# Two-layer experts over memory attention: token matmuls with layer-1 columns on partitions, 32x32 VectorE transposes and tiled sums

## The chip, the cores and the metric

The kernel runs on one core of one Trainium2 chip. The metric is the device time of one execution in microseconds (us). The engines are named as in the profile: PE is TensorE's matmul side and PEld its weight load, DVE is VectorE, ACT is ScalarE, POOL is GpSimd, SP the engine that issues all DMAs here.

## The reference, cut to what matters

Three stages follow each other. For 4 batches of 576 tokens, 8 heads of width 64 and 32 memory slots:

```
a    = softmax over tokens of phi                         # [b,h,s,m]
k_m  = a^T k ; v_m = a^T v                                # [b,h,m,d]
attn = softmax over m of (q k_m^T / 8)                    # [b,h,s,m]
x    = attn v_m, heads side by side                       # [2304, 512]
p    = domain_probs / sum                                 # [2304, 4]
x2   = sum over 4 experts e of p[:,e] * (relu(x w1[e]) w2[e])      # w1 512x1024, w2 1024x512
L    = x2 phi2                                            # [2304, 32] logits of 32 slots
d    = softmax of L over tokens ; c = softmax of L over slots
slot = d^T x2                                             # [32, 512]
out  = c (per slot group of 4: relu(slot v1) v2)          # 8 slot experts, v1 512x1024, v2 1024x512
```

Everything is 32-bit. The kernel never forms x or x2. It multiplies v_m into w1 first (G = v_m w1, per batch and 512 of the 4096 layer-1 columns), so that relu(x w1) is relu(attn G) with a contraction of 256; and it multiplies w2 into phi2 (M), so that the logits are h M and the slot inputs are (d^T h) w2, with h the layer-1 outputs times p.

## The kernel before, in words

The order of instructions on every engine is the order in which the Python code issues them. The main loop walks over 4 batches and 8 chunks of 512 layer-1 columns (32 steps). Each chunk is half of an expert.

- `g_half` (L381) makes G for the next step, 256 rows at a time: four matmuls whose results lie on four groups of 32 partitions (column tiles), contraction 128 with half of `vb` zero. ACT writes the rounded value (`hi`), DVE the rest (`lo`).
- `up` (L402) makes h for a tile of 128 tokens: tokens on partitions, 512 columns; six matmuls (A hi x G hi, A hi x G lo, A lo x G hi, for two halves of the contraction) into one of two PSUM banks (`psm`, tag `mm`). A batch has five such tiles; the fifth holds its last 64 tokens beside 64 zero columns. DVE takes the bank out with relu and the token's share p (L423).
- `turn` (L430) turns the previous step's h tile with four TensorE transposes and an ACT copy (L444), since `logits` (L446) needs columns on partitions. `logits` adds up over all 8 chunks of a batch in PSUM.
- `group` (L556) ends a batch: softmax statistics over tokens, transposes back to tokens on partitions (`back`), weighted sums over tokens (`sums`, L620, four column tiles of 32 at a time), and the row softmax for the output (`row_exp`, `row_norm`, `row_turn`).
- `attention(b)` (L789) makes the next batch's `A`, `kbd` and `vb`. Its pieces and those of `group` stand in a list `bg`, from which `pump` takes one entry after each `up`. In batch 0 the steps also hold `m_stages`, which makes M from w2.
- After the last batch come 160 blocks of 256 KB: 32 of w2 again, 64 of v1, 64 of v2. They are fetched in a fixed order (`order`) by SP as slots come free: 56 slots (`blk`), shared with h, G, q, k, v and output tiles, some kept back by `reserve` in the last batch. `fold` and `combine` make the two halves of the output.

Of the kernel before, what the change touches and what calls it, by code (L numbers as in the profile page):

```python
# [16 lines left out]
def kernel(  # L17
# [17 lines left out]

    nc = tc.nc
# [7 lines left out]
    NB = 56  # L44
# [4 lines left out]
    hTp = ctx.enter_context(tc.tile_pool(name="hTp", bufs=1))  # L49
    rawp = ctx.enter_context(tc.tile_pool(name="rawp", bufs=2))  # L50
    blk = ctx.enter_context(tc.tile_pool(name="blk", bufs=NB))
# [10 lines left out]
    live = [0]  # L62

    def block(shape, name, dt=F32):

        live[0] += 1
        assert live[0] <= NB, (name, live[0])
        return blk.tile(shape, dt, tag="b", name=name)

    def spent(n=1):  # L70
        live[0] -= n
        fill()
# [6 lines left out]
    par = const.tile([128, 2], F32)  # L79
# [3 lines left out]
    prob = const.tile([128, 18, E], F32)  # L83
    ct = const.tile([128, 18, 128], F32R)
    A = [const.tile([128, 2, 2, 640], F32R, name=f"A{n}") for n in range(2)]
    kbd = [const.tile([128, 4, 2, NM], F32, name=f"kbd{n}") for n in range(2)]
    vb = [const.tile([128, 2, 128], F32, name=f"vb{n}") for n in range(2)]
    M = const.tile([128, NCH, 4, NSLOT], F32)
    srun = const.tile([128, 2, 512], F32)
# [7 lines left out]
    def load_phi(b):  # L97

        t = att.tile([128, 36, NM], F32, tag="ph", name="ph")
        nc.sync.dma_start(  # L100
            out=t[:, 0:32, :].rearrange("p (h r) m -> p h (r m)", h=H),
            in_=phi[b, :, 0:512, :].rearrange("h (p r) m -> p h (r m)", r=4),
        )
        for c in range(2):
            nc.sync.dma_start(
                out=t[64 * c:64 * c + 64, 32:36, :],
                in_=phi[b, 4 * c:4 * c + 4, 512:576, :].rearrange("i p m -> p i m"),
            )
        ph_t[b] = t

    def load_kv(b, w):

        src = (k, v)[w]
        if w == 0:
            kv_t[b, "t"] = att.tile([128, 2, 4, HD], F32, tag="kt", name="kt")
        t = kv_t[b, "t"]
        for c in range(2):
            nc.sync.dma_start(
                out=t[64 * c:64 * c + 64, w],
                in_=src[b, 4 * c:4 * c + 4, 512:576, :].rearrange("i p d -> p i d"),  # L120
            )
        for c in range(2):
            for ih in range(2):
                t = block([128, 2, 4 * HD], "kv")
                h0 = 4 * c + 2 * ih
                nc.sync.dma_start(
                    out=t,
                    in_=src[b, h0:h0 + 2, 0:512, :].rearrange("i (p r) d -> p i (r d)", r=4),
                )
                kv_t[b, w, c, ih] = t  # L130

    def load_q(b, ti):

        t = block([128, 4, 2, HD], "q")
        for c in range(2):
            if ti < 4:
                nc.sync.dma_start(
                    out=t[:, :, c],
                    in_=q[b, 4 * c:4 * c + 4, 0:512, :].rearrange("i (p r) d -> r p i d", r=4)[ti],
                )  # L140
            else:
                nc.sync.dma_start(
                    out=t[0:64, :, c],
                    in_=q[b, 4 * c:4 * c + 4, 512:576, :].rearrange("i s d -> s i d"),
                )
        q_t[b, ti] = t

    def kv_stages(b):
# [57 lines left out]
        def whole(w, c):  # L206

            def f():
# [3 lines left out]
                for r in range(5):  # L212
                    for i in range(4):
                        o = st[w, c][32 * i:32 * i + 32, 0:64]
                        if r < 4:
                            nc.tensor.matmul(  # L216
                                o, main(c)[:, i, r, :],
                                kv_t[b, w, c, i // 2][:, i % 2, r * HD:(r + 1) * HD],
# [7 lines left out]
                spent(2)  # L226
# [16 lines left out]
        def sk():  # L243
            sums()
            km = att.tile([128, 2, 64], F32, tag="mx", bufs=2, name="km")
            for c in range(2):
# [5 lines left out]
            st["rp"] = att.tile([128, 2, 2], F32, tag="rsp", name="rsp")  # L252
            nc.vector.tensor_tensor(
                out=st["rp"], in0=st["rs"].unsqueeze(2).to_broadcast([128, 2, 2]),
                in1=par.unsqueeze(1).to_broadcast([128, 2, 2]), op=ALU.mult,
            )

# [11 lines left out]
        def vs(c):  # L269
            def f():  # L270
                whole(1, c)()
                if c == 0:
                    st["vm"] = att.tile([128, 2, 128], F32, tag="vm", name="vm")
                for g in range(2):
                    nc.scalar.activation(
                        out=st["vm"][:, c, 64 * g:64 * g + 64], in_=st[1, c][:, 0:64],
                        func=ACTF.Copy, scale=st["rp"][:, c, g:g + 1],
                    )
            return f

        def s6():

            t5 = bank()
            for c in range(2):
                nc.tensor.transpose(t5[:, 128 * c:128 * c + 128], st["vm"][:, c, :], ident)
            nc.scalar.copy(  # L286
                out=vb[b % 2], in_=t5[:, 0:256].rearrange("p (c m) -> p c m", c=2)
            )
# [3 lines left out]
    def q_stages(b, ti):  # L292
# [3 lines left out]
        o = 128 * ti if ti < 4 else 512 + 64 * (b % 2)  # L296

        def s0():
            t = bank()
            for j in range(4):  # L300
                nc.tensor.transpose(
                    t[:, 128 * j:128 * j + n], q_t[b, ti][0:n, j].rearrange("p c d -> p (c d)"),
                    ident[0:n, 0:n],
                )
            spent()
            qt = att.tile([128, 4, 128], F32, tag="qt", bufs=2, name="qt")
# [59 lines left out]

    raw = {}

    def load_w1(s):
        if s >= B * NCH:  # L370
# [8 lines left out]
    G = {}  # L379

    def g_half(s, c):  # L381

        def f():
            b = s // NCH
            t = bank()
            for i in range(4):
                nc.tensor.matmul(  # L387
                    t[32 * i:32 * i + 32, :], vb[b % 2][:, c, 32 * i:32 * i + 32],
# [669 lines left out]
```

## Time and profile before

| | us |
|---|---|
| median of 3 runs (lowest, highest) | 707.61 (706.89, 713.17) |
| the profiled execution | 708.74 |
| its span, first to last instruction | 707.0 |
| PE busy in it | 641.8 |
| DVE busy | 303.0 |
| ACT busy | 198.2 |

The profile is one execution. Times in its views count from the first instruction; a line of a timeline gives start, length, engine, source line, operation, tiles (written <- read), shapes and how many were merged, then in brackets how long the engine had been idle and what ended that. A matmul of 32-bit operands that is not rounded first shows as two records.

### The profile page before, as it was taken

The numbers are of one execution on the slowest core, as the hardware profiler recorded it, in microseconds if no ns is written. First come the engines' busy times: TensorE is split into PE (matmuls) and PEld (weight loads), VectorE is DVE, ScalarE is ACT, GpSimd is POOL, SyncE is SP. The second block draws the span as 40 slices with busy tenths as digits, with TensorE's granted clock in tenths as the row PEclk, the third lists the DMA queues.
The fourth block names the chain that finished last, engine by engine and source line by source line (L and its number), as shares of the span: only waits on it lengthen the run. The fifth ranks groups of instructions, "written<-read, shape, count | busy, mean of one in ns | idle before, by whom it ended". The sixth has DMA issues, their size and how long they took to land.

```text
span 707.0 us, 11204 instructions
## 1 busy us (share of the span) xinstructions
PE 641.8 (91%) x4588; PEld 376.6 (53%) x4588; DVE 303.0 (43%) x655; ACT 198.2 (28%) x438; POOL 2.2 (0%) x11
## 2 busy tenths in 40 slices
PE   7969999999999999899999999999899987899995
PEld 6746675666554566555545566564555553222232
DVE  4576456444443634633345645633533331311012
ACT  1323343333341323323313323322222223010012
POOL 0000000000000000000000000000000000000000
PEclk7999999999999999999999999999999998999997
DMA  7856432331115522111111553232312322999999
GB/s 213 256 171 217 151 127 84 139 136 60 61 61 160 156 76 83 60 60 60 61 59 60 160 158 98 62 117 92 133 60 75 119 62 103 379 404 388 382 382 311
DMA packets 97554, 105.95 MB, mean 150 GB/s; under 512 B 31456, under 2 KB 64736, under 8 KB 97504
## 3 DMA queue, kind: packets, MB, share of 16 engines
q1 hardware_dynamic: 97504, 105.24, 45.0%
q8 instruction: 36, 0.59, 0.3%
q14 instruction: 14, 0.11, 0.0%
HBM read 100.50 MB, written 4.72 MB: 149 GB/s over the span
## 4 chain that ended last, share of the span: by engine, by line
PE 72%; DMA 11%; ACT 8%; DVE 6%; issue 1%; SPq 0%; ACTq 0%; DVEq 0%
PE mm L411 11%; PE mm L412 10%; PE mm L413 10%; DMA v<-in_moe_w_dram 9%; PE at L387 9%; PE at L435 7%; PE lb L454 6%; PE at L620 5%; ACT hT L444 3%; ACT g L392 3%; DMA ph<-in_phi_dram 2%; PE at L316 2%; PE at L478 2%; PE at L216 1%; ACT hTx L444 1%
## 5 line engine op out<-in xcount | busy, mean ns | idle before, releaser
L423 DVE TENSOR_SCALAR h<-mm,prob 128x512 f32<-128x512 f32 (+1 forms) x160 | 119.9, 749 | 159.2 <-PE mm L413 156.3
L411 PE MATMUL mm<-g,A 128*128 128x512 f32 x320 | 142.4, 445 | 0.5 <-ACT A L349 0.5
L412 PE MATMUL mm<-g,A 128*128 128x512 f32 x320 | 126.8, 396 | 0.0
L413 PE MATMUL mm<-g,A 128*128 128x512 f32 x320 | 126.3, 395 | 0.0
L444 ACT COPY hT<-at 128x512 f32<-128x512 f32 x128 | 74.8, 587 | 125.4 <-PE at L435 125.4
L435 PEld LDWEIGHTS at<-ident,h 128*128 128x128 f32 x576 | 66.6, 140 | 62.2 <-issue 38.9
L435 PE MATMUL at<-ident,h 128*128 128x128 f32 x576 | 89.2, 278 | 0.1
L411 PEld LDWEIGHTS mm<-g,A 128*128 128x128 f32 x320 | 60.9, 190 | 33.9 <-issue 12.4
L387 PE MATMUL at<-raw,vb 128*32 128x512 f32 x512 | 68.6, 608 | 0.2 <-ACT vb L286 0.2
L413 PEld LDWEIGHTS mm<-g,A 128*128 128x128 f32 x320 | 60.3, 188 | 14.8 <-DVE A L350 0.2
L392 ACT CAST g<-at 128x512 fp32r<-128x512 f32 x64 | 37.5, 586 | 102.7 <-PE at L387 102.6
L412 PEld LDWEIGHTS mm<-g,A 128*128 128x128 f32 x320 | 61.0, 191 | 8.2 <-issue 0.7
L393 DVE TENSOR_TENSOR g<-at,g 128x512 fp32r<-128x512 f32 x64 | 44.2, 690 | 45.8 <-ACT g L392 45.5
L454 PE MATMUL lb<-hT,M 128*32 128x512 f32 x256 | 34.1, 605 | 22.2 <-ACT hT L444 22.2
L1013 PE MATMUL mm<-v,hz 128*8 128x256 f32 x256 | 35.7, 380 | 3.7 <-DVE mm L937 1.3
L620 PE MATMUL at<-h,dt 128*32 128x512 f32 x288 | 35.2, 630 | 0.3 <-ACT dt L611 0.3
L910 PE MATMUL mm<-v,sT 128*32 128x512 f32 x128 | 28.7, 600 | 0.9 <-DMA v<-in_moe_w_dram 0.5
L484 DVE COPY w2T<-at 128x128 f32<-128x128 f32 x64 | 17.9, 290 | 16.9 <-ACT w2T L486 16.7
L444 ACT COPY hTx<-at 128x512 f32<-128x512 f32 x16 | 9.4, 585 | 53.6 <-PE at L435 53.6
L1013 PEld LDWEIGHTS mm<-v,hz 128*8 128x8 f32 x256 | 8.6, 87 | 27.8 <-DMA v<-in_moe_w_dram 19.2
L316 PE MATMUL at<-kbd,qt 128*128 128x64 f32 (+1 forms) x160 | 19.7, 266 | 3.0 <-ACT qt L307 2.3
L387 PEld LDWEIGHTS at<-raw,vb 128*32 128x32 f32 x512 | 10.1, 108 | 22.9 <-issue 17.1
(145 smaller groups left out, 494.7 us busy)
## 6 DMA issues: line engine op xcount, KB each, us to landing
v<-in_moe_w_dram SPq DMA_DIRECT2D x160, 256.0 KB, 5.4
raw<-in_moe_w_dram SPq DMA_DIRECT2D x32, 1024.0 KB, 5.0
w<-in_moe_w_dram SPq DMA_DIRECT2D x32, 256.0 KB, 5.3
kv<-in_k_dram SPq DMA_DIRECT2D x16, 256.0 KB, 4.3
q<-in_q_dram SPq DMA_DIRECT2D x32, 128.0 KB, 5.0
kv<-in_v_dram SPq DMA_DIRECT2D x16, 256.0 KB, 4.8
out_dram<-ot SPq DMA_DIRECT2D x16, 256.0 KB, 4.1
ph<-in_phi_dram SPq DMA_DIRECT2D x4, 512.0 KB, 6.7
```

What stands on the lines that cost most here:

```text
L387: nc.tensor.matmul(t[32 * i:32 * i + 32, :], vb[b % 2][:, c, 32 * i:32 * i + 32], raw[s][:, 2 * c + i // 2, :], start=True, stop=True,)
L392: nc.scalar.copy(out=hi, in_=t)
L393: nc.vector.tensor_tensor(out=lo, in0=t, in1=hi.bitcast(F32), op=ALU.subtract)
L411: nc.tensor.matmul(ps, ah, gh, start=(c == 0), stop=False)
L412: nc.tensor.matmul(ps, ah, gl, start=False, stop=False)
L413: nc.tensor.matmul(ps, al, gh, start=False, stop=(c == 1))
L423: nc.vector.tensor_scalar(out=hid[T, n][rows], in0=ps[rows], scalar1=0.0, scalar2=prob[rows, T, e:e + 1], op0=ALU.max, op1=ALU.mult,)
L435: nc.tensor.transpose(t[:, 128 * a:128 * a + 128], hid[T, n][:, 128 * a:128 * a + 128], ident)
L444: nc.scalar.copy(out=dst, in_=t.rearrange("p (a t) -> p a t", a=4))
L454: nc.tensor.matmul(lb[key][32 * a:32 * a + 32, 0:w], M[:, n, a, :], src[:, a, :], start=(n == 0), stop=(n == NCH - 1),)
L620: nc.tensor.matmul(t[32 * j:32 * j + 32, :], st["dt"][:, i], hid.pop((T0 + i, 4 * kk + j)), start=(i == 0), stop=(i == nt - 1),)
L1013: nc.tensor.matmul(acc[32 * i:32 * i + 8, :], hz[:, eb, g * fp + f, i, :], use((2, dh, eb, fp, i))[:, n_ * f:n_ * f + n_], start=(k_ == 0 ...
```

## The change

Layer-1 columns go on partitions. `up` now takes 128 columns of G as weights and streams 288 tokens (half a batch, no zero columns) of A: 8 groups of six matmuls a step. ACT takes the bank out with relu into `hT`, which `logits` reads as it is; DVE copies it to `hid` in transposed 32x32 blocks. The share p no longer goes into h: `logits` closes after each expert, DVE transposes its 32x32 blocks, POOL (for the last expert DVE) multiplies by the share and adds up (`expert`), and the weights of the sums get it too (`weights`). `sums` uses 32x32 tiles of TensorE: 4 groups of token rows into 4 PSUM banks, 4 experts on 4 groups of columns. `g_mult` puts the two halves of G on two groups of 64 rows, without zeros. The last batch goes in two halves (`units`), so that its first half's tokens are finished early; the fetches go into whole tiles that become free (`A0`, `ph`, five `big` ones of nine blocks, `A1`, `raw`, `g`), and output tiles share five `hT` slots. Before the first `up`, all of batch 0's q tiles are now done.

```diff
-    blk = ctx.enter_context(tc.tile_pool(name="blk", bufs=NB))
+    gp = ctx.enter_context(tc.tile_pool(name="gp", bufs=2))
+    bigp = ctx.enter_context(tc.tile_pool(name="bigp", bufs=5))
+    units = [(b, ((0, 288), (288, 576))) for b in range(B - 1)]
+    units += [(B - 1, ((0, 288),)), (B - 1, ((288, 576),))]
...
+    def g_mult(s):
...
+        ts = [bank() for c in range(2)]
+        for i in range(4):
+            for c in range(2):
                 nc.tensor.matmul(
+                    ts[c][32 * i:32 * i + 32, :], vb[b % 2][64 * c:64 * c + 64, 32 * i:32 * i + 32],
+                    raw[s][64 * c:64 * c + 64, i, :], start=True, stop=True,
+                )
...
+    def up(u, n, fb, ki):
...
+        ps = mbank()[:, 0:w]
         for c in range(2):
-            nc.tensor.matmul(ps, ah, gh, start=(c == 0), stop=False)
-            nc.tensor.matmul(ps, ah, gl, start=False, stop=False)
-            nc.tensor.matmul(ps, al, gh, start=False, stop=(c == 1))
-        nc.vector.tensor_scalar(
-            out=hid[T, n][rows], in0=ps[rows], scalar1=0.0, scalar2=prob[rows, T, e:e + 1],
-            op0=ALU.max, op1=ALU.mult,
-        )
+            ah, al = A[b % 2][:, c, 0, o0:o1], A[b % 2][:, c, 1, o0:o1]
+            gh, gl = g[:, 2 * c, f0:f0 + 128], g[:, 2 * c + 1, f0:f0 + 128]
+            nc.tensor.matmul(ps, gh, ah, start=(c == 0), stop=False)
+            nc.tensor.matmul(ps, gh, al, start=False, stop=False)
+            nc.tensor.matmul(ps, gl, ah, start=False, stop=(c == 1))
+        if ki == 0:
+            hT[u, n, fb] = hTp.tile([128, S], F32, tag="hT", name="hT")
+        t = hT[u, n, fb]
+        nc.scalar.activation(out=t[:, o0 - base:o1 - base], in_=ps, func=ACTF.Relu)
+        if ki == len(ranges) - 1:
+            nc.vector.transpose(
+                out=hid[u, n // 2][:, 4 * (n % 2) + fb], in_=t[:, 0:o1 - base]
+            )
-    def turn(b, n, ti):
...
+        def expert(e):
+            lt = pc.tile([128, nt, 32], F32, tag="lt", name="lt")
+            for ki, (o0, o1) in enumerate(ranges):
+                nc.vector.transpose(
+                    out=flat(lt)[:, o0 - base:o1 - base], in_=lb.pop((u, ki))[:, 0:o1 - o0]
+                )
+            eng = nc.vector if e == E - 1 else nc.gpsimd
...
+        def weights():
+            dt_ = pc.tile([128, nt, 32], F32, tag="lt", name="dt")
+            nc.vector.transpose(out=flat(dt_), in_=flat(st["lc"]))
...
+            for e in range(E):
+                (nc.gpsimd if e == 0 else nc.vector).tensor_tensor(
+                    out=we[:, :, e], in0=dt_, in1=share(e), op=ALU.mult
+                )
...
+        def sums():
+            ts = [bank() for _ in range(4)]
+            for tb in range(nt):
+                for e in range(E):
+                    for p in range(4):
+                        rows = slice(32 * p, 32 * p + 32)
                         nc.tensor.matmul(
+                            ts[p][32 * e:32 * e + 32, 0:256], st["we"][rows, tb, e],
+                            hid[u, e][rows, :, tb], start=(tb == 0), stop=(tb == nt - 1),
                         )
...
+        for u, (b, ranges) in enumerate(units):
...
+                if u == NU - 2 and n == 0:
+                    fill(const, "A0", 4, again=False)
+                    fill(att, "ph", 2, again=False)
+                if u == NU - 1 and n == 0:
+                    for _ in range(5):
+                        fill(bigp, "big", 9)
...
+                for fb in range(4):
+                    for ki in range(len(ranges)):
+                        up(u, n, fb, ki)
+                        if gs:
+                            gs.pop(0)()
+                        if fb == 0 and ki == 0 and last is not None:
+                            lu, ln = last
+                            logits(lu, ln)
+                            if ln % 2:
+                                groups[lu][0](ln // 2)
+                                if ln == NCH - 1:
+                                    bg[:0] = [[f] for f in groups[lu][1]]
...
+                        if fb == 1 and ki == 0 and s + 1 < NG and u < NU - 1:
+                            gs = g_mult(s + 1)
+                    if mi:
+                        mi[1 + fb]()
+                    pump()
...
+                if mi:
+                    mi[5]()
+                    mi[6]()
...
+                ot = hTp.tile([128, 2, n_], F32, tag="hT", name="ot")
```

The list that `groups[lu][1]` names is `whole`, `stats`, `weights`, `sums`, `row_exp`, `row_norm`: `whole` is a TensorE sum of the experts' parts and an ACT copy, `stats` a DVE transpose, maximum and an ACT exponential.

## Rows read from the trace of the kernel before

**Rows 1.** The profile's page: PE's busy time and its granted clock in 40 slices.
```profile
PE 641.8 (91%) x4588; PEld 376.6 (53%) x4588; DVE 303.0 (43%) x655; ACT 198.2 (28%) x438; POOL 2.2 (0%) x11
...
PEclk7999999999999999999999999999999998999997
```

**Rows 2.** Busy time by stretch: last batch's steps, then the fetched blocks.
```profile
460.00:582.00 122.00, 112.27 (x697) 67.41 (x694) 45.91 (x72) 33.10 (x60) 0.00 (x0) 1.00 0.28 95
617.00:707.00 90.00, 77.23 (x453) 24.90 (x453) 13.46 (x39) 9.96 (x19) 0.00 (x0) 0.96 1.04 374
```

**Rows 3.** Timeline of PE, one `turn`, one `up`, one `g_half`.
```profile
300.73 0.60 PE L435 MATMUL at<-ident,h 128*128 128x128 f32 x4
301.09 0.48 PE L411 MATMUL mm<-g,A 128*128 128x512 f32 x1
301.40 0.39 PE L412 MATMUL mm<-g,A 128*128 128x512 f32 x1
...
302.33 0.40 PE L413 MATMUL mm<-g,A 128*128 128x512 f32 x1
302.66 1.06 PE L387 MATMUL at<-raw,vb 128*32 128x512 f32 x8
303.66 0.66 PE L435 MATMUL at<-ident,h 128*128 128x128 f32 x4
```

**Rows 4.** Timeline of PE, rounded matmuls that stream 256 columns, two and four.
```profile
688.35 0.50 PE L974 MATMUL cb<-sr,ct 128*128 128x256 f32 x2
...
696.00 0.73 PE L974 MATMUL cb<-sr,ct 128*128 128x256 f32 x4 [0.93 <-DVE sr L958]
```

**Rows 5.** Groups of instructions by line and shape: busy us, mean ns.
```profile
L444 ACT COPY hT<-at 128x512 f32<-128x512 f32 x128 | 74.8, 587 | 125.4 <-PE at L435 125.4
L484 DVE COPY w2T<-at 128x128 f32<-128x128 f32 x64 | 17.9, 290 | 16.9 <-ACT w2T L486 16.7
L486 ACT COPY w2T<-at 128x128 f32<-128x128 f32 x64 | 16.3, 268 | 14.5 <-DVE w2T L484 14.1 <-PE at L478 0.5
L980 DVE COPY ot<-cb 128x512 f32<-128x512 f32 x10 | 6.9, 692 | 18.9 <-PE cb L974 18.9
L917 ACT ACTIVATE hs<-mm,rz 128x512 f32<-128x512 f32 x4 | 2.7, 687 | 30.0 <-PE mm L910 24.7 <-DMA v<-in_moe_w_dram 5.3
```

**Rows 6.** Waits: who waited for whom, us in total, times, longest.
```profile
PE lb L454 <- ACT hT L444: 22.2, 32, 1.0
...
PE lb L454 <- ACT hTx L444: 11.5, 16, 0.7
```

**Rows 7.** Timeline of PE, `logits` and the `up` behind it.
```profile
523.66 1.07 PE L454 MATMUL lb<-hT,M 128*32 128x512 f32 x8 [0.68 <-ACT hT L444]
524.66 0.50 PE L411 MATMUL mm<-g,A 128*128 128x512 f32 x1
```

**Rows 8.** Chain of waits, sixteen matmuls of `sums` (thirty-two records).
```profile
351.82 3.57 PE at L620 x32
```

**Rows 9.** Timeline of SP: when the 160 blocks were asked for.
```profile
541.10 59.94 SPq L659 DMA_DIRECT2D v<-in_moe_w_dram  x25
601.12 42.58 SPq L662 DMA_DIRECT2D v<-in_moe_w_dram  x64
644.58 43.32 SPq L670 DMA_DIRECT2D v<-in_moe_w_dram  x64
688.13 5.10 SPq L985 DMA_DIRECT2D out_dram<-ot  x8
```

**Rows 10.** Chain of waits, the last block's landing.
```profile
687.48 5.32 DMA v<-in_moe_w_dram
```

**Rows 11.** Timeline of PE: memory keys first used, first `up` of steps 0 and 1.
```profile
20.56 1.08 PE L316 MATMUL at<-kbd,qt 128*128 128x64 f32 x8 [0.48 <-DVE kbd L264]
...
29.94 0.48 PE L411 MATMUL mm<-g,A 128*128 128x512 f32 x1
...
56.62 0.78 PE L411 MATMUL mm<-g,A 128*128 128x512 f32 x1
```

More of the change, by code (lines that the diff above doesn't have):

```diff
@@ L60, in mbank, with big @@
         return psm.tile([128, 512], F32, tag="mm", name="mm")
[L62 to L72, printed above, removed]
+    def big(shape, name, dt=F32):
+        return bigp.tile(shape, dt, tag="big", name=name)
     ident = const.tile([128, 128], F32)
@@ L121, in load_kv @@
             )
         for c in range(2):
[L123 to L130, printed above, removed]
-    def load_q(b, ti):
[L134 to L146, printed above, removed]
+            nc.sync.dma_start(
+                out=kv_t[b][:, w, c],
+                in_=src[c, :, 0:512, :].rearrange("i (p r) d -> p i (r d)", r=4),
+            )
@@ L283, in s6 @@
             t5 = bank()
[L284 to L288, printed above, removed]
+            nc.tensor.transpose(t5[:, 0:128], st["vm"].rearrange("p c d -> p (c d)"), ident)
+            nc.scalar.copy(out=vb[b % 2], in_=t5[:, 0:128])
         return [s0, s1, s2, whole(0, 0), whole(0, 1), sk, s5, vs(0), vs(1), s6]
@@ L379 @@
     G = {}
[L381 to L386, printed above, removed]
+    pair = [None]
+    def g_mult(s):
+        b, n = divmod(s, NCH)
+        if b < B - 1 or n < 2:
+            t = gp.tile([128, 4, FH], F32R, tag="g", name="g")
+        else:
+            if n % 2 == 0:
+                pair[0] = big([128, 2, 4, FH], "g", F32R)
+            t = pair[0][:, n % 2]
+        G[s] = t
+        ts = [bank() for c in range(2)]
+        for i in range(4):
+            for c in range(2):
@@ L632, in sums, with row_exp @@
-            return f
-        return [
-            [own], [stats], [back], [sums(0)], [sums(1)], [lambda: row_norm(st, nt)],
-            [lambda: row_turn(st, T0, nt)],
-        ]
-    order = [("w", kk, a, j) for kk in range(2) for a in range(4) for j in range(4)]
+        def row_exp():
+            lr = st["lr"]
+            mx = pc.tile([128, NT], F32, tag="cmx", name="cmx")[:, 0:nt]
+            nc.vector.tensor_reduce(out=mx, in_=lr, axis=AX.X, op=ALU.max)
+            nc.vector.tensor_tensor(
+                out=lr, in0=lr, in1=mx.unsqueeze(2).to_broadcast([128, nt, 32]), op=ALU.subtract
+            )
+            nc.scalar.activation(out=lr, in_=lr, func=ACTF.Exp)
@@ L641 @@
+        return expert, [whole, stats, weights, sums, row_exp, row_norm]
+    order = [("w", kk, j) for kk in range(8) for j in range(4)]
     order += [(1, eb, nn, c, i) for eb in range(2) for nn in range(2) for c in range(4) for i in range(4)]
@@ L648 @@
     nxt = [0]
-    reserve = [None]
     def fetch(t):
@@ L676, in fetch, with fill @@
         blkv[key] = t
-    def fill():
-        if reserve[0] is None:
-            return
-        while live[0] + reserve[0] < NB and nxt[0] < len(order):
-            fetch(block([128, 512], "v"))
     held = {}
-    def fill_pool(pool, tag, n, **kw):
+    def fill(pool, tag, n, again=True, **kw):
         n = min(n, len(order) - nxt[0])
@@ L865 @@
+        lu, ln = last
+        logits(lu, ln)
+        groups[lu][0](ln // 2)
+        wb[0] = mbank()
+        fill(const, "A1", 4, again=False)
+        gl = groups[lu][1]
+        for f in gl[:4]:
+            f()
+        for _ in range(2):
+            fill(rawp, "raw", 4)
+        for _ in range(2):
+            fill(gp, "g", 4)
+        rest = gl[4:]
         rz = pc.tile([128, 1], F32, tag="rz", name="rz")
```

588 lines of the change are left out of this document (268 added, 320 removed).

## The prediction

> **What bounds the kernel now.** I read the page first: PE is busy for 641.8 of 707 us and its granted clock stays at the upper level, 2.4 GHz, in nearly every slice, so a step costs what PE's queue costs [rows 1]. The stretches say that this holds for the steps (112 of 122 us busy in the last batch, with DMA at 0.28), and that the end is another regime: from 617 on the DMA engines are full, and PE's busy time there is time that follows the blocks [rows 2]. So the change needs two sums: PE's time for the 32 steps, and from where the block stream then runs. DVE and ACT have room on average, which says nothing of who waits in a given place.
>
> **PE's time, part by part** (us over the whole run; minus is gained).
>
> *up.* One call now is 0.31 to its second matmul (it comes behind another kind of matmul), four distances of 0.2325, and 0.23 to what follows: 1.47 [rows 3]; 160 calls make 235. After, there are 1536 matmuls of 288 columns. Two more of 256 columns cost 0.73 - 0.50 = 0.23, so 0.115 each [rows 4]; 512 columns cost 0.2325 [rows 3]; on the line between them 288 cost 0.130. That is 200, and 6 for 72 returns from other kinds of matmul (0.08 each, 0.31 less 0.23). Change -29. The weights are loaded 1.6 times as often; the 256-column row carries that load already. Bounds 0.115 to 0.15: 177 to 230.
>
> *turn.* 0.36 from its first transpose to the next `up` [rows 3], 144 times: -52.
>
> *G.* A `g_half` takes 1.00 to the next operation and 0.10 to get in (302.33 + 0.23 to 302.66) [rows 3]; 64 of them, 70. `g_mult` does two in one if the two groups of 64 rows work side by side, as the four column groups of one `g_half` visibly do: 35. Change -35; bound 0.
>
> *logits.* Now 1.0 [rows 7] 32 times, and 16 tails of a quarter as many columns (0.36, estimated from that row): 38; and PE waits 22.2 + 11.5 for ACT's copy of the turned tile [rows 6]. After, the relu of the last tile has one `up` of 0.78 (6 x 0.13) to land in, so the wait goes; 64 sets of four matmuls, 288/512 of 0.86, are 31, and 40 visits 0.24 each for getting in and out, 10. Change -31.
>
> *sums.* Sixteen matmuls take 3.57 with some 0.14 for getting in and out [rows 8], so four column tiles of 512 columns 0.86, and 36 such sets 31. After, 72 sets of sixteen 32x32 tiles with 256 columns. If all sixteen overlap, a set costs 0.43 and the sum is again 31: no change. No row shows two groups of rows at once. With eight at a time it is 62 (+31), with four at a time 124 (+93). I take the first, because the column groups of the same array overlap fully in rows 3 and 8.
>
> The Trainium skill (TensorE: Matmul & The Clock Gate, Part 3: Packing small matmuls) says that tiles in different row and column groups run at once and gives 10.6 for sixteen tiles of 512 columns; no run here shows it yet. An estimate by that figure is 0.43 x 16/10.6 for a set, 47 in all, 16 above mine.
>
> *back, row_turn.* 36 transposes of about 0.11: -4.
>
> *Start.* Memory keys are first used at 20.56 and the first `up` starts at 29.94 [rows 11]. All five q tiles now come before it. DVE's price grows by about 1.04 ns a column (0.29 at 128, 0.69 at 512 [rows 5]), so 0.42 at 256; a q tile is five such operations and two small ones, 2.5, and five tiles 12.4, with the rest of the chain and G's remainders to about 39: +9. In return step 0, which takes 26.7 (29.94 to 56.62 [rows 11]) with three tiles in it, loses some 8 of that. Net +1.
>
> **New waits on PE.** The bank of `up` is now emptied by ACT in its queue's order. A relu of 288 columns costs 0.40 (268 ns at 128, 587 at 512 [rows 5]); the last matmul's results are there about 0.17 after its streaming (0.40 long, 0.23 to the next [rows 3]), so with two banks a slot comes back 1.44 after it was taken, where PE wants it after 1.56. The slack is 0.12: whatever stands ahead of a relu in ACT's queue stops PE. I price these places, as estimates from rows 5:
> - a batch end: `whole` waits for the last expert's DVE chain (two transposes at 0.46, a product and a sum of 576 columns at 0.76, less one `up`): 1.7; ACT stands at the exponential of `stats` behind a transpose and a maximum: 1.3; `sums` waits for transpose and products: 1.7; `row_exp` stands behind the four updates of `srun`: 1.3. Six for each of three batches, three for the half: 21.
> - `attention`, where ACT stands at exponentials behind DVE's maximum and subtraction: some 0.7 for each of eight rounds, 6 a batch: 18.
> - `m_stages`: `part` and `fold` are now called in a row, with only ACT's copy (0.59) and its queue between: 1.1 eight times, 9. Before, an `up` lay between them.
> - the two `hi` casts of a step: 0.15, 32 times: 5.
>
> Together +53; bounds 20 and 85. DVE's transposes of 576 columns, at a copy's price 0.76 four times a step, lie beside PE's 9 us step; no row has this operation. POOL's products have a whole expert's time to hide in.
>
> Sum for the steps: -29 - 52 - 35 - 31 - 4 + 1 + 53 = -97. The last `up` ends at about 485 where it ended at 582 [rows 2].
>
> **The end.** Of the 160 blocks (256 KB), 128 are asked for in 86.8 us, 0.678 each [rows 9]; before 541 only seven had been. After: six go into `A0` and `ph` in the first half of the last batch. The second half is eight rounds of 3.9 (24 x 0.13 and 0.8 for logits) and 7.5 for the first half's end: 39, so it begins at 446. Its `big` tiles come free in three ways: two when `sums` of the first half is done (about 10 in), one each when G's pairs are used up (chunk 3 at about 469, chunk 5 at 477, chunk 7 at 485). SP stands in order at each fill, but nothing else is in its queue. From 477 the stream has no gap, and 33 blocks are through: 127 x 0.678 = 86, to 563; the last lands 5.3 later [rows 10], 568. PE's chain (second half's end at 485, its statistics and sums some 14, w2 7) is done before 510 and then follows the blocks, as now. From the last landing to the end it is now 14.2 (687.48 + 5.32 to 707.0). Ten output tiles of each half share five slots and wait for landings, where there were plenty: +4, estimated at most of one landing. End of span 587; outside it lie 708.74 - 707.0 = 1.7: **588**. The profiled execution is 1.1 above the median, which I leave in.
>
> **The rivals.**
> - *Half the tiles overlap.* `sums` takes 62: the steps end 31 later and so does all: 619. For it: nothing shows sixteen at once. Against: four column tiles cost no more than one would, 3.57 / 16 = 0.22 a matmul of two records [rows 8], where one record of as many columns takes 0.23 alone [rows 3].
> - *Row groups exclude each other (slower than before).* Place: `sums` and `g_mult`. With four at a time, +93 and +35: 716. Worse, because the order takes the row groups in the inner loop, neighbours would always exclude each other and nothing overlaps: 1152 x 0.43 = 495. It decides as soon as the two cost 120 more than in my sum. Against it speaks only that the same array runs column groups at once, which is no proof for rows.
> - *ACT is the bound.* If a relu costs like the other activation from PSUM, 687 ns and not shorter for fewer columns [rows 5], a slot comes back after 1.73, and each of 256 calls pays 0.09: +22, and the waits above grow to their upper bound, +32: 642 together, 610 with the first alone. For it: the slack of 0.12. Against: the copies in rows 5 do shrink with their columns.
> - *Fewer waits.* ACT and DVE catch up during one wait for the next, and only 20 of the 53 remain: 555.
> - *The turning is only moved.* If DVE's transpose takes four times a copy's time, a step needs 4 x 3.0 + 1.4 = 13.4 of DVE where PE needs 9; 32 x 4.4 = 141 is given back, less some 25 of the waits, which it swallows: 704. For it: no row has the operation. Against: nothing in a copy of a row's length hints at it.
>
> **How the numbers follow.** Forecast 0.50; half the tiles 0.14; ACT 0.13; fewer waits 0.13; row groups 0.06; DVE 0.04. The forecast's own unknown prices move it by -23 to +30 (`up`) and -33 to +32 (waits). Below 545 lies only the corner where both are low, above 650 lie the row groups, the DVE case and the corner where both are high with half the tiles; together under 2 in 10, so the range is 545 to 650. Within 1% (701 to 715; a measurement of this kernel tells no less apart) lies most of the DVE case, 0.03; slower the row groups, 0.06; the rest is faster, 0.91.
>
> **What would show it.** In the profile after: matmuls of `up` 0.13 apart; `g_mult` about 1.1 in all; a set of sixteen in `sums` 0.43; no turn lines; waits of PE on ACT's relu near batch ends and in `attention`, on ACT's copy before `fold`; blocks streaming without gap from about 477. I am wrong if `sums` takes over twice its 31, if the distance in `up` is set by something other than columns, if PE's waits exceed 85, or if the stream starts much later than the last half.

## The result and the profile after

The changed kernel takes 690.19 us (median of 4 runs, 685.96 to 697.27), the kernel before 708.4: ratio 0.9712, 95% interval 0.9634 to 0.979. The ratio leaves out the run of 697.27, which counts as slow beside the others, and so isn't that of the medians. The changed kernel is 18 us faster where 120 were forecast. The profiled execution took 691.91, its span is 690.1. The last `up` ends at 572.05 (583 before, 485 forecast).

From the page of the changed kernel: busy time, granted clock in 40 slices, groups (busy, mean ns | idle before).

```profile
PE 571.0 (83%) x6750; PEld 396.3 (57%) x6750; DVE 310.0 (45%) x663; ACT 196.8 (29%) x478; POOL 35.3 (5%) x39
...
PEclk9989998899979999979899999989998898899995
...
L425 PE MATMUL mm<-A,g 128*128 128x288 f32 x512 | 174.7, 341 | 13.7 <-ACT hT L431 12.7
L431 ACT ACTIVATE hT<-mm 128x288 f32<-128x288 f32 x256 | 104.2, 412 | 264.6 <-PE mm L427 264.1
...
L596 PE MATMUL at<-h,we 32*32 32x256 f32 x2304 | 60.0, 449 | 25.4 <-POOL we L585 15.4
```

PE's work did fall, by 71 us against [rows 1]. But PE now stands idle for 119 us where it was 65, and its clock is no longer full. By stretch, batches 0 to 2 and the two halves of the last one:

```profile
35.00:185.00 150.00, 126.53 (x1134) 97.91 (x1133) 69.08 (x153) 54.19 (x126) 6.41 (x5) 0.93 0.42 134
185.00:315.00 130.00, 112.78 (x1473) 84.76 (x1473) 67.45 (x126) 41.61 (x106) 8.17 (x6) 0.91 0.33 98
315.00:441.00 126.00, 107.99 (x1468) 81.60 (x1467) 68.52 (x129) 41.92 (x108) 8.16 (x6) 0.95 0.34 101
441.00:523.00 82.00, 64.22 (x954) 40.86 (x953) 37.76 (x73) 21.39 (x52) 5.39 (x6) 0.92 0.25 85
523.00:572.00 49.00, 43.40 (x552) 35.95 (x550) 24.84 (x60) 14.38 (x38) 4.61 (x6) 0.90 0.56 192
```

The granted clock (the number behind the five engines) is 0.90 to 0.95 where it was 1.00 in the last batch of before [rows 2]. From 36 to 572 PE has 34 gaps of over 0.9 us; before it had three. Added up over windows of 1 us from 35 to 600, PE spent 95.6 us at the lower level, 1.2 GHz (13.5 before). Half of PE's busy time in them, 42 us, is an estimate of what that cost (6 before): it takes all of that work to run at half speed.

A step without extras takes 9.0 (14.7 before); the step behind a batch's end takes 36.0, 34.3 and 33.6, and 19.6 between the two halves of the last batch. The end of the second batch on PE's timeline:

```profile
315.28 0.29 PE L427 MATMUL mm<-A,g 128*128 128x288 f32 x1
315.51 1.18 PE L448 MATMUL lb<-hT,M 128*32 128x288 f32 x16
316.61 0.40 PE L425 MATMUL mm<-A,g 128*128 128x288 f32 x1
316.85 0.30 PE L426 MATMUL mm<-A,g 128*128 128x288 f32 x1
316.98 0.29 PE L427 MATMUL mm<-A,g 128*128 128x288 f32 x1
...
318.99 1.21 PE L543 MATMUL at<-acc,rr 128*128 128x288 f32 x4 [1.31 <-DVE acc L535]
...
320.93 1.09 PE L384 MATMUL at<-raw,vb 64*32 64x512 f32 x16
...
328.13 0.40 PE L425 MATMUL mm<-A,g 128*128 128x288 f32 x1 [3.52 <-ACT hT L431]
...
329.35 0.44 PE L425 MATMUL mm<-A,g 128*128 128x288 f32 x1
329.58 0.44 PE L426 MATMUL mm<-A,g 128*128 128x288 f32 x1
...
332.55 6.59 PE L596 MATMUL at<-h,we 32*32 32x256 f32 x244 [1.57 <-POOL we L585]
339.83 2.76 PE L596 MATMUL at<-h,we 32*32 32x256 f32 x128 [0.69 <-issue]
343.56 2.76 PE L596 MATMUL at<-h,we 32*32 32x256 f32 x128 [0.97 <-issue]
347.01 1.96 PE L596 MATMUL at<-h,we 32*32 32x256 f32 x76 [0.70 <-issue]
```

Four things are to be seen. A matmul of `up` comes 0.13 after the one before it, but 0.23 to 0.24 at each change of kind (315.28 to 315.51, 316.61 to 316.85). PE waits 1.31, 3.52 and 1.57 at the stages of `group`. Behind the waits the matmuls are 0.23 to 0.24 apart everywhere: the clock. And `sums` (L596) takes 16.4, not 7.8, and pauses after every 128 records with nothing to wait for. Windows show the clock:

```profile
324.00:328.00 4.00, 0.61 (x5) 0.38 (x3) 2.60 (x6) 1.26 (x5) 0.00 (x0) 1.00 0.64 245
329.00:332.00 3.00, 1.99 (x9) 1.64 (x7) 3.00 (x7) 0.82 (x2) 1.23 (x1) 0.50 0.00 0
336.00:339.00 3.00, 3.00 (x156) 2.33 (x144) 0.00 (x0) 0.00 (x0) 0.00 (x0) 1.00 0.02 5
```

PE idles from 324.6 to 328.1, the clock is at 0.50 from 328.6 to 335.5, and it rises while `sums` is running. The 3.52 is ACT standing at the exponential of `stats` ahead of a relu in its queue; DVE's chain ends at 326.7:

```profile
326.74 0.77 ACT L568 ACTIVATE lc<-lc,nm 128x576 f32<-128x576 f32 x1 [2.79 <-DVE nm L567]
...
327.70 0.39 ACT L431 ACTIVATE hT<-mm 128x288 f32<-128x288 f32 x1
```

The end, SP's DMA issues (start, length, count):

```profile
542.63 17.09 SPq L651 DMA_DIRECT2D v<-in_moe_w_dram  x26
559.76 56.80 SPq L654 DMA_DIRECT2D v<-in_moe_w_dram  x64
616.91 47.82 SPq L662 DMA_DIRECT2D v<-in_moe_w_dram  x64
```

and what SP waited for from 500 on (in total, times, longest):

```profile
SPq L651 <- PE at L596: 39.6, 1, 39.6
...
SPq L654 <- PE at L596: 8.5, 1, 8.5
SPq L654 <- PE mm L427: 7.7, 2, 3.9
SPq L651 <- PE mm L427: 2.7, 1, 2.7
```

The last half begins at 523.2 (forecast 446). The stream starts at 542.6, when the `sums` of the first half are done: 19 into the last half, not 10, and it has gaps where none were forecast from 477 on. It takes 122 for 154 blocks, 0.79 each, against 0.678 [rows 9].

### The profile page after: what moved, and what is told of

The parts are those of the page before. It is cut to its first block, busy times and chain, and to the rows that moved or that the text cites. A ratio compares the mean times of both kernels' runs of the same rounds, so it can differ in the third digit from the quotient of the medians.

```text
span 690.1 us, 15584 instructions
## 1 busy us (share of the span) xinstructions
PE 571.0 (83%) x6750; PEld 396.3 (57%) x6750; DVE 310.0 (45%) x663; ACT 196.8 (29%) x478; POOL 35.3 (5%) x39
## 4 chain that ended last, share of the span: by engine, by line
PE 55%; DVE 17%; DMA 11%; ACT 7%; issue 6%; SPq 2%; POOL 1%; ACTq 0%; DVEq 0%; POOLq 0%
PE mm L425 10%; PE at L596 9%; PE mm L427 8%; DMA v<-in_moe_w_dram 8%; PE mm L426 7%; PE lb L448 6%; PE at L384 4%; DVE g L395 3%; DVE h L433 3%; ACT hT L431 3%; PE at L495 1%; PE mm L882 1%; DMA out_dram<-ot 1%; PE at L471 1%; PE at L485 1%
## 5 line engine op out<-in xcount | busy, mean ns | idle before, releaser
L425 PE MATMUL mm<-A,g 128*128 128x288 f32 x512 | 174.7, 341 | 13.7 <-ACT hT L431 12.7
L431 ACT ACTIVATE hT<-mm 128x288 f32<-128x288 f32 x256 | 104.2, 412 | 264.6 <-PE mm L427 264.1
L433 DVE STREAM_TRANSPOSE h<-hT 128x576 f32<-128x576 f32 (+1 forms) x160 | 104.4, 654 | 156.0 <-ACT hT L431 155.5
L427 PE MATMUL mm<-A,g 128*128 128x288 f32 x512 | 158.3, 309 | 7.7 <-DVE g L395 7.3
L426 PE MATMUL mm<-A,g 128*128 128x288 f32 x512 | 157.0, 307 | 0.0
L425 PEld LDWEIGHTS mm<-A,g 128*128 128x128 f32 x512 | 101.8, 199 | 67.7 <-ACT hT L431 33.4
L427 PEld LDWEIGHTS mm<-A,g 128*128 128x128 f32 x512 | 101.9, 199 | 11.2 <-DVE g L395 10.5
L426 PEld LDWEIGHTS mm<-A,g 128*128 128x128 f32 x512 | 102.6, 200 | 0.4
L596 PE MATMUL at<-h,we 32*32 32x256 f32 x2304 | 60.0, 449 | 25.4 <-POOL we L585 15.4
L596 PEld LDWEIGHTS at<-h,we 32*32 32x32 f32 x2304 | 41.6, 112 | 43.2 <-POOL we L585 17.0
L448 PE MATMUL lb<-hT,M 128*32 128x288 f32 x512 | 45.2, 460 | 0.0
L384 PE MATMUL at<-raw,vb 64*32 64x512 f32 x512 | 38.9, 627 | 0.1
L300 PEld LDWEIGHTS at<-kbd,qt 128*128 128x128 f32 (+1 forms) x160 | 17.8, 180 | 8.0 <-ACT qt L291 6.9
L448 PEld LDWEIGHTS lb<-hT,M 128*32 128x32 f32 x512 | 13.7, 118 | 14.8 <-issue 8.8
```

What stands on the lines that cost most here:

```text
L300: nc.tensor.matmul(sc[0:n, :, j, :], st["qt"][:, j, 0:n], kbd[b % 2][:, j], start=True, stop=True)
L384: nc.tensor.matmul(ts[c][32 * i:32 * i + 32, :], vb[b % 2][64 * c:64 * c + 64, 32 * i:32 * i + 32], raw[s][64 * c:64 * c + 64, i, :], star ...
L425: nc.tensor.matmul(ps, gh, ah, start=(c == 0), stop=False)
L426: nc.tensor.matmul(ps, gh, al, start=False, stop=False)
L427: nc.tensor.matmul(ps, gl, ah, start=False, stop=(c == 1))
L431: nc.scalar.activation(out=t[:, o0 - base:o1 - base], in_=ps, func=ACTF.Relu)
```

## The experiments

Three theories came from the timeline above: the clock behind waits, instruction supply in `sums`, and the places of ACT's and DVE's work in the order. Ratios are to the kernel before, measured beside each run. The last two columns are of the profiled execution alone. It can lie well off the median (e3_spread 11 above it, e8_fold_late2 9 below it), and its first `up` starts anywhere from 35 to 39.5; so differences of some 4 us in the last column tell nothing.

| run | built on | median us | ratio (95%) | profiled us | last `up` ends |
|---|---|---|---|---|---|
| e1_fill | changed | 715.6 | 1.0075 (1.0045 to 1.0104) | 714.83 | 591 |
| e1b_fill_half | changed | 683.35 | 0.9625 (0.9556 to 0.9695) | 680.28 | 560 |
| e2_half_cols | changed | 695.42 | 0.9779 (0.9713 to 0.9845) | 699.87 | 581 |
| e4_fold_late | changed | 688.14 | 0.9683 (0.9644 to 0.9723) | 689.3 | 570 |
| e3_spread | changed | 669.35 | 0.9387 (0.9336 to 0.9437) | 680.82 | 562 |
| e5_half_g2 | e3 | 667.97 | 0.9403 (0.9338 to 0.9468) | 663.0 | 545 |
| e6_chunks | e3 | 697.14 | 0.9811 (0.9766 to 0.9855) | 700.85 | 577 |
| e7_att_exp | e3 | 655.02 | 0.9145 (0.906 to 0.9229) | 653.64 | 535 |
| e8_fold_late2 | e7 | 628.7 | 0.8783 (0.8727 to 0.8839) | 619.7 | 502 |
| e9_chunk16 | e7 | 653.75 | 0.9217 (0.9171 to 0.9263) | 656.44 | 539 |
| e10_outq | e7 | 656.6 | 0.9277 (0.9234 to 0.9321) | 657.69 | 534 |
| e11_all | e8, e9, e10, e5 | 631.1 | 0.884 (0.8789 to 0.8891) | 630.97 | 509 |
| e13_best | e8, e5 | 623.77 | 0.875 (0.8705 to 0.8794) | 625.1 | 506 |
| e15_fill | e13 | 622.68 | 0.8725 (0.8673 to 0.8777) | 621.39 | 500 |

### The clock: e1_fill, e1b_fill_half

```diff
+    def hold(t, n):
+        for _ in range(n):
+            nc.tensor.matmul(t[:, 0:128], ident, ident, start=True, stop=True)
```

It is called in the bank that comes next ahead of L543, behind `stats`, and ahead of `sums`, `part` and `fold`.

> Matmuls without use (ident by ident, about 0.11 us each at full clock) stand where PE waits anyway: 10 before the token sum of the logits, 28 after the statistics, 14 before the weighted sums, 12 and 6 before the two steps of the M chain in batch 0. No wait is taken away. Theory 1 (each wait of PE is paid a second time, because the granted clock falls to half behind it): the stretches at clock 0.50 behind batch ends and in batch 0 go; they cost PE 27 us in the changed kernel's trace (4.0+2.6+1.6+2.1+1.6+2.8+2.5 at batch ends, 3.4+3.3+1.7+1.7 in batch 0), so the time falls from 690 to 663 to 670. Rival (the clock falls for another reason, or the added matmuls only lengthen the waits): 688 to 700, with the same stretches at 0.50.

> As e1_fill, with half as many added matmuls (5, 14, 7, 6, 3): in e1_fill's trace one took 0.21 to 0.23, not 0.11, so that 28 outlasted the wait of 3.5. The kernel is otherwise the changed one. Theory 1 (the waits let the granted clock fall, which costs PE a second time): now the fillers fit into the waits; the time at half clock goes from 96 to under 60 us, the layer-1 matmuls cost 10 to 17 less, the whole 668 to 680. Rival (the fall is worth nothing, since what follows PE is late anyway): 685 to 700.

e1_fill raised the clock (13 us lost to it by the same estimate, instead of 42) and cost more than that: between the first and the last `up` its matmuls took 81 us where 41 of waits went, and PE's other work 25 less. e1b_fill_half, timeline of PE at the same batch end:

```profile
312.87 3.29 PE L511 MATMUL at<-ident 128*128 128x128 f32 x28
...
322.57 5.96 PE L608 MATMUL at<-h,we 32*32 32x256 f32 x253 [0.99 <-POOL we L596]
328.70 2.74 PE L608 MATMUL at<-h,we 32*32 32x256 f32 x128 [0.17 <-issue]
```

The clock stays full here. From 35 to 600, 35.2 us at the lower level are left, 17 us lost. The added matmuls took 44 for 36 of waits, PE's other work 20 less (`up` 242 instead of 251), and the last `up` ends 12 earlier. The median is 7 lower where 10 to 22 were expected, and its interval overlaps the changed kernel's (0.9634 to 0.979). So the trace shows that matmuls put into the waits keep the clock up and make the work behind them shorter; that the whole gets faster by it isn't shown. And `sums` still takes 14.5 at full clock: the clock isn't its reason.

### Instruction supply: e2_half_cols, e6_chunks, e9_chunk16

```diff
...
-   hid[u, e][rows, :, tb], start=(tb == 0), stop=(tb == nt - 1),
+   hid[u, e][rows, 0:4, tb], start=(tb == 0), stop=(tb == nt - 1),
...
```

> The 32x32 tiles of the weighted sums take 128 of their 256 columns, the other half of the sums is left at zero; the number of instructions is the same. Theory 2 (a set of sixteen tiles is held by how fast PE gets its instructions, 0.61 a set and a pause every 128 matmuls): the sums of a full batch end stay at 15 to 16.5 us, the time at 683 to 692. Rival (the tiles overlap only in part, so columns are the bound): a set halves, the sums of a full batch end take 9 to 11, and the time falls by some 20 to 25, to 665 to 670.

Timeline of PE in e2_half_cols at the same batch end:

```profile
342.18 5.18 PE L596 MATMUL at<-h,we 32*32 32x128 f32 x244 [2.04 <-POOL we L585]
348.32 1.90 PE L596 MATMUL at<-h,we 32*32 32x128 f32 x128 [0.96 <-issue]
352.05 1.90 PE L596 MATMUL at<-h,we 32*32 32x128 f32 x128 [1.83 <-issue]
355.78 1.32 PE L596 MATMUL at<-h,we 32*32 32x128 f32 x76 [1.83 <-issue]
```

A group of 128 starts 3.73 after the one before it, with 256 columns (339.83 to 343.56) as with 128 (348.32 to 352.05); only its pause grows, from 0.97 to 1.83. `sums` takes 14.9 instead of 16.4, and the whole is no faster (695, above the 683 to 692 of theory 2, and far from its rival's 665 to 670). So the columns aren't the bound of groups that come one behind another. Each record has its weight load, so 128 are 256 instructions, and the DMA view of the changed kernel from 330 to 349 has nothing but

```profile
DMA packets 4, 0.07 MB, mean 3 GB/s; under 512 B 0, under 2 KB 0, under 8 KB 0
...
q8 instruction: 4, 0.07, 1.3%
```

four packets of the instruction queue, as many as groups. The Trainium skill (Runtime: NRT & Kernel Launch, Instruction fetch mechanics) says that an engine's instructions come in blocks of 16 KB, 256 instructions, and that crossing a block is mostly hidden. The trace agrees with the first (0.07 MB in four); the second doesn't hold here, with 0.7 to 1.0 of pause per block. In the trace's packet records each of these groups starts 1.3 to 1.6 behind the arrival of such a packet, with 256 columns and with 128 alike (arrivals at 338.24, 342.16 and 345.62 in the changed kernel, at 347.00, 350.66 and 354.37 in e2_half_cols). That the packets cause the pauses was not tried by itself.

```diff
-   ts = [bank() for _ in range(4)]        # e6: two banks a pass, eight tiles a set, in portions
+   st["ts"] = [bank() for _ in range(2)]
...
-   bg[:0] = [[], [w_], [s_], [x_], [v_], [], [], [m_], [e_], [n_]]
+   bg[:0] = [[], [w_], [s_], [x_], [v_], [], [m_(0, 6)], [m_(12, 18)], [e_], [n_]]   # e9
+   mid.append(m_(6, 12))
```

> On top of e3_spread: the weighted sums go in two passes of two PSUM banks each (eight tiles a set), and at the two full batch ends and the last in-loop half end in two or three portions with layer-1 matmuls between. The columns and the number of instructions stay. Theory 2 (instruction supply: 128 matmul records each 3.45 to 3.73 us however many columns): while layer-1 matmuls run, which need few instructions, supply gets ahead; sums and their pauses cost 10 to 12 at a full batch end instead of 15.5, the whole 5 to 10 less than e3_spread. Rival (tiles overlap badly: eight at a time is half the speed of sixteen): a set of sixteen goes to 0.85 or more, sums cost 16 to 20, the whole 0 to 15 more.

> On top of e7_att_exp: sixteen tiles a set as in the changed kernel, but in portions (6, 6, 6 sets at full batch ends, 10 and 8 at the first half, 5 and 4 at the second) with layer-1 matmuls between. Theory 2 (instruction supply is the limit of sums, and it gets ahead while layer-1 matmuls run): step with the sums falls from 24.5 to 17 to 20 at a full batch end, the whole by 8 to 14, to 641 to 647. Rival (the supply has no store that fills meanwhile, or the matmuls between stand in the same supply): same pauses, 650 to 657.

e6_chunks, PE's timeline at the ends of the second and the third batch, and a window of the latter:

```profile
338.14 5.41 PE L607 MATMUL at<-h,we 32*32 32x256 f32 x192
...
439.75 31.61 PE L607 MATMUL at<-h,we 32*32 32x256 f32 x576 [1.54 <-POOL we L591]
```

```profile
440.00:450.00 10.00, 10.00 (x181) 7.85 (x181) 1.37 (x3) 0.00 (x0) 0.00 (x0) 0.50 0.02 3
```

Without the last matmul's own length of 0.37, a set of eight takes (5.41 - 0.37) / 12 = 0.42 and one of sixteen, in the changed kernel between pauses, (2.76 - 0.37) / 4 = 0.60. Two passes cost 0.84, as the rival said. So more than eight overlap, and eight are no cheaper than the 0.43 that I had put for sixteen. With its pauses a set of sixteen comes to 0.85 as well (15.4 for 18 in e3_spread): the pauses eat what the sixteen gain. And 36 sets of eight in a row ran at half clock, 0.88 a set, for over 30 us although PE had no gap. That is most of the 28 that the whole lost against e3_spread (the rival had 0 to 15): the step with these sums takes 42.9 instead of 26.4.

e9_chunk16 fails too. The pauses put down to "issue" do shrink at the two full batch ends, from 2.2 and 3.1 in e7_att_exp to 0.6 and 1.2. But behind their first four records the sums now wait 1.2 and 1.0 for DVE's remainder of G, and the matmuls between bring changes of kind; the step with the sums is 25.4, not 17 to 20, and 24.4 without the portions.

### Places in the order: e3_spread, e7_att_exp, e4_fold_late, e8_fold_late2, e5_half_g2

```diff
-   bg[:0] = [[f] for f in groups[lu][1]]
+   w_, s_, x_, v_, m_, e_, n_ = groups[lu][1]      # x_: the exponentials, cut from stats
+   if len(ranges) > 1:
+       bg[:0] = [[], [w_], [s_], [x_], [v_], [], [], [m_], [e_], [n_]]
+   else:
+       bg[:0] = [[w_], [s_], [x_], [v_], [m_], [e_], [n_]]
```

> At a batch end the exponentials of the statistics are issued one place later than their maximum, and between the stages stand more pairs of layer-1 matmuls (first an empty place, then token sum, maximum, exponentials, weights, two empty places, sums); the two half ends get the separate exponentials only. Theory (ACT standing at the exponentials behind DVE's chain stops the layer-1 matmuls, and the stages follow each other too closely): the waits of 1.3, 3.5 and 1.6 us at each of the two full batch ends go, and the stretches at clock 0.50 behind them, 4.0 and 2.6: together some 19, 668 to 675. Rival (the waits only move on to the next stage, since the chain of DVE and ACT behind it is as long): 685 to 692.

```diff
-   return [s0, s1, s1b, s2]                        # order=((2, 2), (1, 1), (0, 0), (3, 3))
+   return [s0, s1, s1x, s1b, s2]                   # order=((4, 4), (2, 2), (3, 3), (1, 1), (0, 0))
```

> On top of e3_spread: in attention the exponential of a q tile goes one row of the order later than the maximum and subtraction that it needs, and the last transposes of the oldest tile come first in a row. Theory (ACT stands at the exponential behind DVE, and the relus queued behind it hold up PE): PE's waits for ACT's relu in the steps with attention go, 3 to 5 us a batch with the clock, the whole 8 to 14 less than e3_spread. Rival (other waits of the row, for DVE's normalisation or the copies, take their place): within 4 of e3_spread.

Both theories hold: 21 and another 14 us. In e3_spread the first two steps of batches 1 and 2 take 36.0 and 34.7 instead of 46.4 and 44.6. In batch 1 of e7_att_exp the last steps with attention take 14.9, 12.1 and 14.7 instead of 18.0, 12.8 and 19.5, and batch 0 147 instead of 155 (153 in e5_half_g2, which has e3_spread's batch 0).

```diff
-   mi[1 + fb]()                     # behind the second up of each fb
...
-   mi[5]()
-   mi[6]()
+   mi[5]()
+   late.append(mi[6])               # called behind the next step's first up; logits one up later
...
+   FLIP = ((1, 1), (2, 0), (2, 1), (3, 0))    # e8; e4: behind the first up of each fb
```

> In batch 0 the four transposes of w2 come one group of layer-1 matmuls earlier, and the last step of M (fold) after the first group of the next step, so that each copy has a group to land in. Theory (PE's waits for these copies are 9.8 + 7.8 us and let the clock fall, 10.1 more): batch 0 takes 125 to 132 instead of 150, the whole 663 to 672. Rival (batch 0 is held by something else, the loads of w2 or attention, and the waits move there): batch 0 145 to 150, the whole 685 to 692.

> On top of e7_att_exp: as e4_fold_late, but the four transposes of w2 stand in the second to last groups of a step, so that its load has three groups more to land. Theory (e4_fold_late took away 17 us of waits for the copies and got 12.4 back as waits for the load of w2, issued at the step's end): without both, batch 0 falls from 147 to 125 to 132, and the whole by 13 to 20 against e7_att_exp, to 635 to 642. Rival (batch 0 is held by a third thing, DMA traffic of 1 MB of w1 and 1 MB of w2 a step, or by PE's own 130): batch 0 140 to 147, the whole within 6 of e7_att_exp.

Waits of PE (in total, times, longest) in batch 0, changed kernel:

```profile
PE at L485 <- DVE w L477: 9.8, 8, 1.5
PE at L495 <- ACT mp L490: 7.8, 8, 2.6
```

and e4_fold_late:

```profile
PE at L471 <- DMA w<-in_moe_w_dram: 12.4, 3, 5.5
...
PE at L485 <- DVE w L477: 0.5, 1, 0.5
```

e4_fold_late took the waits away and gained nothing (batch 0 151, the intervals of both ratios overlap): the transposes, now earlier, meet the load of w2. With the load given its time, e8_fold_late2 brings batch 0 to 120 and the whole down by 26, more than expected; 7 us are then lost to the clock in the whole run.

```diff
-   if fb == 1 and ki == 0 and s + 1 < NG and u < NU - 1:
+   if fb == (0 if u == NU - 2 and n >= 2 else 1) and ki == 0 and s + 1 < NG and u < NU - 1:
```

> On top of e3_spread: in the first half of the last batch, from its third step on, the next step's G is made one group of layer-1 matmuls earlier. Theory (a round there takes 6.7 instead of 5.3, because the low part of G reaches PE too late by DVE's queue): rounds fall from 6.7 to 5.3 to 5.8, five of them, so the whole falls by 5 to 7 against e3_spread. Rival (ACT's and DVE's work per round is the bound, not its start): rounds stay at 6.6 to 6.7.

The rounds fall from 6.7 to 5.7 and the half batch by 5, as expected; the medians can't tell it (0.9403 against 0.9387).

### The end, and all together: e10_outq, e11_all, e13_best, e15_fill

```diff
-   nc.sync.dma_start(
+   (nc.sync if dh else nc.scalar).dma_start(
        out=out[b * S:b * S + 512, d0:d1]...
```

> On top of e7_att_exp: the first half of the output goes out by ACT's DMA queue, not SP's. Theory (in SP's queue these ten tiles stand behind the last fetches of v2, their five slots come free only after them, and the second half's fold waits: 24 from the last block to the end instead of 14.2): the tail falls to 14 to 18, the whole by 5 to 9, to 646 to 650. Rival (the output's 2.4 MB then compete with the blocks, and the last block comes as much later): 653 to 658.

> All together: e7_att_exp with the M chain of e8, the portions of e9, the output queue of e10 and the earlier G of e5_half_g2. If the causes are the ones named and add up: 655 less 16, 10, 7 and 5: 612 to 625. If they share the same microseconds (the clock behind the waits, the end that follows the blocks): 630 to 645.

The rival of e10_outq holds. SP's last 64 blocks in e7_att_exp and in e10_outq:

```profile
578.64 47.50 SPq L671 DMA_DIRECT2D v<-in_moe_w_dram  x64
```

```profile
578.41 54.17 SPq L671 DMA_DIRECT2D v<-in_moe_w_dram  x64
```

What the output sends earlier, the blocks lose. e11_all gains nothing over e8_fold_late2, since two of its four parts were worth nothing. Left out, they make e13_best; e15_fill adds `hold` with 7 at the half ends and ahead of the third batch's `sums`.

> e8_fold_late2 with the earlier G of e5_half_g2 in the first half of the last batch, without the portions and the output queue of e11_all, which gained nothing. Theory (the rounds of 6.7 are held by G's low part, and the block stream starts as much earlier as the last half does): rounds 5.6, the whole 4 to 7 less than e8_fold_late2, 621 to 625. Rival (the end is bound by slots and by DMA, so an earlier last half changes nothing): 626 to 631.

> e13_best with seven matmuls without use (0.21 each) ahead of the token sum at the two half ends and ahead of the weighted sums at the end of the third batch and of both halves, where PE still waits 1.5 to 4.1. Theory (the sums that follow run at half clock only because PE waited): the last stretches at clock 0.50 go, 4 to 6 us of PE's time, the whole 2 to 6 less than e13_best. Rival (instruction supply sets the pace of the sums at either clock, and the end follows the blocks): within 2 of e13_best.

e13_best: rounds 5.7, as far below e8_fold_late2 as expected, but the intervals overlap. e15_fill: 21.2 us at the lower clock instead of 37.6, and `sums` are busy for 51.5 instead of 55.1, so the clock does count in them; the time is within 2, as its rival said. These two are 12.5% and 12.75% faster than the kernel before.

## Why the prediction was wrong

The sign and most mechanisms were right, the sum for the steps was not: from the first to the last `up` 537 us where 446 were forecast, and the last `up` ends 87 late. PE's starts on the timeline, summed by line and with each idle time put to what ended it, give the terms:

- *up* (forecast 206, measured 251). The distance is 0.133, so 204 for 1536. The term "72 returns, 0.08 each" failed: there are 141 visits of another kind, and each costs 0.19 (0.24 to get in, 0.22 to get out, less two of 0.13): 27. Of the other 20 about 15 are the clock (118 of its matmuls start at the lower level, 90 of them some 0.24 from the next); the rest lies right beside waits.
- *sums* (27 for the 63 sets before the last `up`; 51 busy and 7 of pauses). This term failed by 31, the most for one cause. That tiles in different groups of rows overlap was right; that all sixteen do at the price of one was not: a set takes 0.60 and not 0.43, and behind the first 244 records each 128 come 3.45 to 3.73 apart, whatever their columns (e2_half_cols). I had counted columns and no instructions: 2304 records where the page of before has 288 (nine times the 32 in rows 8). The figure that the prediction takes from the Trainium skill (TensorE: Matmul & The Clock Gate, Part 3: Packing small matmuls), 47 in all by its estimate, was nearer than mine, and still short of the 60 busy and 9 of pauses in the whole run.
- *New waits* (53). 82 idle less the 7 above and less 9.5 that were there before: 66, in the bounds of 20 to 85. ACT behind `stats` was named, but at 1.3; it is 3.5. The waits for DVE's copy of w2's transposes in batch 0 (9.8) and for the half batch's G (rounds 6.7; 5.7 in e5_half_g2) were not named.
- *The clock* had no term at all. The prediction read the full clock of before as given [rows 1], but PE had hardly a gap there. The waits that I added bring it down, and behind many of them the work then takes longer too. It is part of the 20 in `up` and of the first part of `sums`; 42 in all by the estimate above, 36 before the last `up`. e1b_fill_half wins back 20 in PE's work and 12 at the last `up`.
- *turn, G, logits* came as forecast: `turn` gone, `g_mult` 1.09 a call and 35.7 in all (35), logits 41.3 (41). Row groups of 64 work side by side. DVE's transpose of 576 takes 0.774 (0.76), the relu 0.412 (0.40):

```profile
L433 DVE STREAM_TRANSPOSE h<-hT 128x576 f32<-128x576 f32 x96 | 74.1, 774 | 111.0 <-ACT hT L431 110.6
```

45 + 31 + 13 make 89 of the 91 that are missing; the rest is spread over small terms. The first `up` came 4 earlier than forecast (35.2, not 39), but at 39.5 in e1_fill and e3_spread, which start alike; executions differ by as much. Of the four signs of being wrong that the prediction names, two came: `sums` over twice its 31, counted with the pauses, and the late stream.

*The end* (103 forecast from the last `up` to the end of the execution, measured 120). The tail behind the last landing was right: 18.2 forecast, 19.4 measured (616.91 + 47.82 and 6.0 to land, to 690.1). The stream without gaps was wrong: it starts 19 into the last half, SP then waits 10.4 until `up` is done with the last chunks of G and 8.5 for the last `sums`, and the last 64 blocks come 0.747 apart (0.677 [rows 9]).

Of the rivals none is the answer. ACT isn't the bound by its rate: PE's waits for its relu, 12.7 in all, fall to 3.7 in e13_best with ACT's work only moved. What a step's places cost is shown by e3, e7 and e8: 61 us between them, with the tiles and columns as they are. e13_best's 624 is still 36 above the forecast: its `sums` take 55 of PE in the whole run and 17 of idle time ahead of them and in their pauses, against 31 forecast for the sums themselves (60 and 25 in the changed kernel). Why 1 KB packets of the last blocks move at 349 GB/s in the changed kernel and at 380 before (DMA view of 617 to 665, and of 645 to 685), though SP waits for the queue in both, stays open.

## What to carry to other kernels

Count instructions as well as columns: tiles of 32x32 make so many that, in long runs of them, fewer columns brought nothing here. A wait that a change puts on TensorE can be paid twice, once as the wait and once at half clock behind it. Work from a neighbouring stage between two stages of a chain took 21 us off here (e3_spread) without making any stage faster. When a wait goes, look at the queue's next entry (here the load of w2) before counting the gain.

## What the runs showed of the hardware

- PE with no gap at all can run at half clock: 30 us in e6_chunks with eight 32x32 tiles at a time. With sixteen at a time the clock rose (336 to 339 above), but in e2_half_cols, with 128 columns and longer pauses, it was at half for the whole of the last `sums`, 10.4 us.
- DVE and POOL slow each other. DVE, POOL and two groups of the changed kernel, in `weights` (L585) and `expert` (L534):

```profile
330.70 0.75 DVE L585 TENSOR_TENSOR we<-dt,pe 128x576 f32<-128x576 f32 x1
...
331.37 1.74 DVE L585 TENSOR_TENSOR we<-dt,pe 128x576 f32<-128x576 f32 x1
...
330.77 1.73 POOL L585 TENSOR_TENSOR we<-dt,pe 128x576 f32<-128x576 f32 x1 [31.82 <-DVE dt L577]
...
L534 POOL TENSOR_TENSOR lt<-lt,pe 128x576 f32<-128x576 f32 x6 | 7.2, 1193 | 194.4 <-DVE lt L526 194.4
...
L534 DVE TENSOR_TENSOR lt<-lt,pe 128x576 f32<-128x576 f32 x3 | 2.3, 758 | 0.1
```

  Of three products on DVE beside one on POOL, the first and the third take 0.75, as alone (0.758); the second takes 1.74, and POOL's 1.73 where it takes 1.19 alone. So the three take 3.1 together; all four on DVE would be 4 x 0.758 = 3.0, and POOL's help is worth nothing. The Trainium skill (GPSIMD Engine Reference, Specifications) says that the two share their way to SBUF, with contention when a DVE instruction has two inputs there; the rows agree.
- A matmul of another kind among those of `up` costs 0.10 on the way back into `up` and 0.09 on the way out (medians of 121 and 102 places at full clock in the changed kernel: 0.236 and 0.219 instead of 0.133).
